# A smaller DMA scratch and a filler tile: the same instructions on SBUF tiles at other addresses

## The chip, the cores and the metric

One Trainium2 chip, one of its cores. The metric is device microseconds of one execution of the kernel; a profile of one execution stands beside the times.

## The reference, cut to what matters

```python
def reference(**kwargs):
    attn_out = _attn_ref(q, k, v, centroids)        # 2 x 8 heads, 768 x 64; a query sees the keys of its own cluster
    x = attn_out.transpose(0, 2, 1, 3).reshape(1536, 512)
    h = x @ w_in;  x = np.maximum(0.01 * h, h) @ w_out          # first MLP, 512 -> 2048 -> 512
    h = x @ w_in2; r = np.maximum(h, 0.0); return (r * r) @ w_out2   # second MLP
```

All in fp32; the weights come in as 64-bit floats.

## The kernel before, in words

**Two stages.** The first 240 us are the attention, unit by unit (`PLAN`, an order written out by hand for every engine). The rest is the two MLPs, `m = 0` and `m = 1`, and fills TensorE alone. The change issues nothing and moves nothing in the order, so what matters is which SBUF tiles the instructions of each stage read.

**The MLP stage.** The hidden width of 2048 is cut into 16 chunks `f` of 128. Each chunk has 1024 weights per partition: 512 of `w_in` and 512 of `w_out`. `decode_pieces(ci)` (`ci = 16 m + f`) loads a chunk into `wraw` (L124), turns it into fp32 on ScalarE and VectorE (`wt`, L131 to L148) and splits it into a high part `wh` (ScalarE, L159) and a low part `wl` (GpSimd, L160), each 128 x 1024 fp32r, 4096 bytes per partition. Three products (high x high, high x low, low x high) make up an fp32 product, so:

- `g1` (L728): for one chunk and one block of 512 tokens, 12 matmuls `h`, with a 128 x 128 slice of `wh` or `wl` as the stationary operand and 512 columns of `xh` or `xl` as the moving one.
- `act`: makes `gh` and `gl` from `h` on ScalarE and VectorE.
- `g2` (L770): 12 matmuls `o`. For `m = 0` a slice of `wh` or `wl` is stationary and `gh` or `gl` moves; for `m = 1` a slice of `gh` or `gl` is stationary and the 512 columns of `wh` or `wl` move.

Chunks go in groups (2, 2, 4, 4, 4 for `m = 0`, four times 4 for `m = 1`); each group runs over three token blocks. `g2` runs two units (`LAG = 2`) behind `g1`, so at a change of groups the two mix: 24 matmuls of the old group and 24 of the new one, by twelves.

**Where the weights lie.** `weights[m, f]` lie in a ring of eight places (`RING = 8`). Chunks with `ci % 8 < 4` go to the pool `wpx`, opened on the right side of SBUF while the attention still runs; the others go to `wpb`, on the left side. So **groups alternate**: four chunks in the upper buffers (`wpx`), four in the lower ones (`wpb`). 8 chunks of 16 in each MLP use the upper ones, which makes 8 x 3 x 24 = 576 matmuls per MLP, 1152 of the 2304 in all.

A pool on the right side grows down from the end of the memory, one on the left up from the DMA scratch and the constants. These are the addresses that the built program has for the tiles that TensorE reads and for a few others (bytes within a partition; "place" is the address modulo 4096):

| tile | side | address before | place |
|---|---|---|---|
| DMA scratch | left | 0 to 16384 | |
| `ident` | left | 16512 | 128 |
| `xh`, `xl` | left | 21600, 46176 | 1120 |
| `hb` (three) | left | 70752 to 107616 | 1120 |
| `gh`, `gl` (three each) | left | 78944 to 91232 | 1120, 3168 |
| lower `wh`, `wl` (four each, 4096 bytes apart) | left | 99424 to 132192 | 1120 |
| `vv` (two) | left | 107616, 113760 | 1120, 3168 |
| `e` (eight) | left | 119904 to 144480 | 1120, 96, 3168, 2144 |
| `eh`, `el` (two each) | left | 144480 to 169056 | 1120, 3168 |
| upper `wh`, `wl` (four each, 4096 bytes apart) | right | 184288 to 217056 | 4064 |
| `ds` | right | 184800 | 480 |
| `spl` (two) | right | 189408, 201696 | 992 |
| `rqk` (two) | right | 213984, 220128 | 992, 3040 |
| `rv` | right | 226272 | 992 |

(The right-side tiles of the attention and the upper weight buffers share their space one after the other, as do the left-side ones.)

All loads and stores are issued by SyncE (`nc.sync.dma_start`); no other engine issues a DMA.

Of the kernel before, what the change touches and what calls it, by code (L numbers as in the profile page):

```python
# [8 lines left out]
F32 = mybir.dt.float32  # L9
# [43 lines left out]
def attention_moe_moe_kernel(  # L53
# [9 lines left out]
    nc = tc.nc  # L63
# [18 lines left out]

    const = ctx.enter_context(tc.tile_pool(name="const", bufs=1))
    xp = ctx.enter_context(tc.tile_pool(name="xp", bufs=1))

    xh = xp.tile([128, HP, NT], F32R, name="xh")
    xl = xp.tile([128, HP, NT], F32R, name="xl")
# [590 lines left out]
    for u in range(-1, NU + 5):  # L678
# [8 lines left out]
        for op in PLAN[FIRST[u] if p == 0 else u % UPP].split():  # L687
            if ":" in op:
                name, lag = op.split(":")
# [5 lines left out]
            else:  # L695
                name, ahead = op.split("@")
# [184 lines left out]
```

## Time and profile before

| | us |
|---|---|
| median of 3 runs | 786.04 |
| lowest, highest | 784.79, 786.47 |
| span of the profiled execution | 782.9 |
| TensorE busy in it | 770.1 (98%) |
| VectorE, ScalarE, GpSimd busy | 532.2, 410.8, 293.4 |

The span runs from the first to the last instruction of the program on the core. Of the profiled execution only the span is recorded, no time as for the runs; the median of the runs is 3.1 us over it, the lowest run 1.9 and the highest 3.6. A busy TensorE is not TensorE at its peak: matmuls overlap, and a matmul's duration in a row (some 390 ns) is longer than the step from its start to the next one's start.

### The profile page before, as it was taken

The numbers are of one execution on the slowest core, as the hardware profiler recorded it, in microseconds if no ns is written. First come the engines' busy times: TensorE is split into PE (matmuls) and PEld (weight loads), VectorE is DVE, ScalarE is ACT, GpSimd is POOL, SyncE is SP. The second block draws the span as 40 slices with busy tenths as digits, with TensorE's granted clock in tenths as the row PEclk, the third lists the DMA queues.
The fourth block names the chain that finished last, engine by engine and source line by source line (L and its number), as shares of the span: only waits on it lengthen the run. The fifth ranks groups of instructions, "written<-read, shape, count | busy, mean of one in ns | idle before, by whom it ended". The sixth has DMA issues, their size and how long they took to land.

```text
span 782.9 us, 11015 instructions
## 1 busy us (share of the span) xinstructions
PE 770.1 (98%) x4147; PEld 665.3 (85%) x4147; DVE 532.2 (68%) x772; ACT 410.8 (52%) x759; POOL 293.4 (37%) x258
## 2 busy tenths in 40 slices
PE   8999999999999999999999999999999999999998
PEld 8899999999988888888888888888888888888886
DVE  5899999999998568775664577487257557533333
ACT  6988988988997563443442343445344234212121
POOL 2989889889765412221220214442022012100000
PEclk9999999999999999999999999999999999999999
DMA  7594574573502223233121113013113103000102
GB/s 224 121 205 110 105 180 108 113 164 78 139 1 93 96 85 108 105 107 108 55 107 54 33 75 108 1 54 108 55 54 108 54 0 108 1 0 1 52 17 95
DMA packets 16005, 66.35 MB, mean 85 GB/s; under 512 B 2704, under 2 KB 2704, under 8 KB 10960
## 3 DMA queue, kind: packets, MB, share of 16 engines
q1 hardware_dynamic: 15952, 65.64, 29.2%
q8 instruction: 33, 0.54, 0.3%
q14 instruction: 20, 0.16, 0.1%
HBM read 44.60 MB, written 3.15 MB: 61 GB/s over the span
## 4 chain that ended last, share of the span: by engine, by line
PE 82%; DVE 12%; ACT 4%; issue 1%; POOL 0%; DVEq 0%; ACTq 0%; POOLq 0%
PE o L770 34%; PE h L728 33%; PE A L451 5%; PE S L353 4%; DVE el L433 4%; PE T L416 4%; DVE nm L376 4%; ACT e L386 2%; DVE xt L473 1%; ACT eh L427 1%; DVE ds L279 1%; PE warm L202 1%; PE ohT L308 1%; DVE m L278 1%; PE S L257 1%
## 5 line engine op out<-in xcount | busy, mean ns | idle before, releaser
L160 POOL TENSOR_TENSOR wl<-wt,wh 128x1024 fp32r<-128x1024 f32 x32 | 77.5, 2423 | 297.1 <-ACT wh L159 246.6
L728 PE MATMUL h<-xl,wh 128*128 128x512 f32 x384 | 150.6, 392 | 0.0
L728 PE MATMUL h<-xh,wl 128*128 128x512 f32 x384 | 150.5, 392 | 0.0
L728 PE MATMUL h<-xh,wh 128*128 128x512 f32 x384 | 150.4, 393 | 0.0
L749 DVE TENSOR_TENSOR gl<-g,gh 128x512 fp32r<-128x512 f32 x96 | 91.6, 954 | 44.1 <-ACT gh L748 44.0
L748 ACT CAST gh<-g 128x512 fp32r<-128x512 f32 x96 | 59.6, 621 | 80.5 <-DVE g L745 42.2
L433 DVE TENSOR_TENSOR el<-T,eh 128x512 fp32r<-128x512 f32 x144 | 94.4, 683 | 5.6 <-ACT eh L427 3.7
L403 POOL TENSOR_SCALAR e<-e,r 128x768 f32<-128x768 f32 x96 | 88.5, 933 | 20.7 <-DVE r L400 13.4
L376 DVE TENSOR_REDUCE nm<-S 128x1 f32<-128x768 f32 x96 | 90.8, 947 | 4.6 <-PE S L257 2.3
L386 ACT ACTIVATE e<-S,nm 128x768 f32<-128x768 f32 x96 | 87.0, 906 | 11.1 <-DVE nm L376 6.8
L353 PE MATMUL S<-hb 128*128 128x384 f32 (+1 forms) x384 | 90.5, 350 | 1.6 <-ACT e L386 1.2
L745 DVE TENSOR_TENSOR g<-t 128x512 f32<-128x512 f32 x48 | 39.5, 822 | 73.3 <-ACT t L744 73.2
L744 ACT ACTIVATE t<-h 128x512 f32<-128x512 f32 x48 | 28.7, 598 | 113.3 <-PE h L728 113.2
L728 PEld LDWEIGHTS h<-xh,wl 128*128 128x128 f32 x384 | 72.3, 188 | 16.1
L728 PEld LDWEIGHTS h<-xl,wh 128*128 128x128 f32 x384 | 72.2, 188 | 16.0
L728 PEld LDWEIGHTS h<-xh,wh 128*128 128x128 f32 x384 | 72.2, 188 | 15.9
L427 ACT CAST eh<-T 128x512 fp32r<-128x512 f32 x144 | 79.4, 586 | 10.6 <-PE T L416 10.2
L451 PE MATMUL A<-eh,vv 128*128 128x256 f32 x288 | 79.5, 307 | 3.0 <-DVE xt L473 3.0
L416 PE MATMUL T<-ident,e 128*128 128x128 f32 x576 | 80.0, 274 | 1.1 <-DVE el L433 1.0
L770 PE MATMUL o<-gh,wl 128*128 128x512 f32 x192 | 75.4, 393 | 0.0
L770 PE MATMUL o<-gl,wh 128*128 128x512 f32 x192 | 75.3, 392 | 0.0
L770 PE MATMUL o<-wh,gl 128*128 128x512 f32 x192 | 75.3, 392 | 0.0
(106 smaller groups left out, 1407.0 us busy)
## 6 DMA issues: line engine op xcount, KB each, us to landing
wraw<-w SPq DMA_DIRECT2D x32, 1024.0 KB, 4.7
hb<-spl SPq DMA_DIRECT2D x14, 576.0 KB, 4.8
hb<-spl SPq DMA_DIRECT2D x42, 192.0 KB, 5.1
rqk<-qk SPq DMA_DIRECT2D x16, 384.0 KB, 4.5
rv<-v SPq DMA_DIRECT2D x8, 384.0 KB, 4.1
out<-ob SPq DMA_DIRECT2D x12, 256.0 KB, 2.1
twice<-qk SPq DMA_DIRECT2D x8, 192.0 KB, 6.0
hb<-st SPq DMA_DIRECT2D x28, 48.0 KB, 2.7
```

Source lines behind the costliest of these rows:

```text
L160: nc.gpsimd.tensor_tensor(out=wl, in0=t, in1=wh.bitcast(F32), op=ALU.subtract)
L353: nc.tensor.matmul(out=s[:, c, 0:HALF], lhsT=hb[0:k, a, i * 128 : (i + 1) * 128], rhs=hb[0:k, b, c * HALF : (c + 1) * HALF], start=(a == 0 ...
L376: nc.vector.tensor_reduce(out=n, in_=s_t[t][:, :, 0:HALF], axis=AX.XY, op=ALU.max, negate=True)
L386: nc.scalar.activation(out=e.rearrange("p (a b) -> p a b", a=2), in_=s_t.pop(t)[:, :, 0:HALF], func=AF.Exp, bias=n_t.pop(t), scale=1.0, ac ...
L403: nc.gpsimd.tensor_scalar(out=e_t[t], in0=e_t[t], scalar1=r_t[t // 2][:, t % 2 : t % 2 + 1], scalar2=1.0, op0=ALU.mult, op1=ALU.mult,)
L416: nc.tensor.transpose(T[:, o : o + 128], e_t[2 * u + b][:, kc * 128 : (kc + 1) * 128], ident)
L427: nc.scalar.copy(out=eh[:, 2 * g : 2 * g + 2, :].rearrange("p a b -> p (a b)"), in_=T_t[u, g])
L433: nc.vector.tensor_tensor(out=el[:, 2 * g : 2 * g + 2, :].rearrange("p a b -> p (a b)"), in0=T_t.pop((u, g)), in1=eh[:, 2 * g : 2 * g + 2, ...
L451: nc.tensor.matmul(out=A, lhsT=w, rhs=m[:, kc, :], start=(kc == 0 and i == 0), stop=(kc == KC - 1 and i == 1),)
L728: nc.tensor.matmul(out=h, lhsT=w[:, ws], rhs=x[:, kk, c], start=(kk == 0 and i == 0), stop=(kk == HP - 1 and i == 2),)
L749: nc.vector.tensor_tensor(out=gl, in0=g, in1=gh.bitcast(F32), op=ALU.subtract)
L770: nc.tensor.matmul(out=outs[o], lhsT=l, rhs=r, start=(first and i == 0), stop=(last and i == 2),)
```

## The change

Two edits. The DMA scratch at address 0 shrinks from 16384 to 4096 bytes per partition, so that every left-side tile lies 12288 bytes (three times 4096) lower. A tile of 736 fp32, 2944 bytes, that nothing writes or reads is allocated first on the right side, so that every right-side tile lies 2944 bytes lower.

```diff
     xp = ctx.enter_context(tc.tile_pool(name="xp", bufs=1))
+    rpad = ctx.enter_context(tc.tile_pool(name="rpad", bufs=1, side="right"))
+    rpad.tile([128, 736], F32, name="rp")
...
-    nc = bacc.Bacc("TRN2", target_bir_lowering=False, num_devices=1)
+    nc = bacc.Bacc("TRN2", target_bir_lowering=False, num_devices=1, dynamic_dma_scratch_size=4096)
```

On each of the five engines the same instructions stand in the same order with the same waits; only addresses differ. In the built program after the change:

| tile | address before, place | address after, place |
|---|---|---|
| every left-side tile | | 12288 lower, same place |
| upper `wh`, `wl` | 184288 to 217056, 4064 | 181344 to 214112, **1120** |
| lower `wh`, `wl` | 99424 to 132192, 1120 | 87136 to 119904, 1120 |
| `ds` | 184800, 480 | 181856, 1632 |
| `spl` | 189408 and 201696, 992 | 186464 and 198752, 2144 |
| `rqk` | 213984 and 220128, 992 and 3040 | 211040 and 217184, 2144 and 96 |
| `rv` | 226272, 992 | 223328, 2144 |

## Rows read from the trace of the kernel before

**Rows 1.** The page: busy time of each engine, granted clock by slice.
```profile
PE 770.1 (98%) x4147; PEld 665.3 (85%) x4147; DVE 532.2 (68%) x772; ACT 410.8 (52%) x759; POOL 293.4 (37%) x258
...
PEclk9999999999999999999999999999999999999999
```
**Rows 2.** Busy time by stretch, first row attention, then groups; us, busy (instructions), clock, DMA.
```profile
20.00:240.00 220.00, 214.68 (x1652) 207.53 (x1651) 205.44 (x368) 194.00 (x432) 185.48 (x177) 1.00 0.53 121
...
322.10:376.20 54.10, 54.10 (x240) 44.80 (x239) 34.03 (x46) 21.52 (x31) 12.02 (x5) 1.00 0.28 98
387.70:443.00 55.30, 55.30 (x240) 44.88 (x239) 30.05 (x40) 17.50 (x26) 7.21 (x3) 1.00 0.16 57
...
719.20:778.50 59.30, 59.30 (x263) 49.12 (x262) 21.53 (x33) 12.18 (x21) 0.00 (x0) 1.00 0.10 36
```
**Rows 3.** Timeline of TensorE, single matmuls: start us, duration us; first of each stretch.
```profile
241.42 0.47 PE L728 MATMUL h<-xh,wh 128*128 128x512 f32 x1
...
268.22 0.40 PE L770 MATMUL o<-gh,wh 128*128 128x512 f32 x1
...
310.98 0.39 PE L728 MATMUL h<-xh,wh 128*128 128x512 f32 x1
...
322.04 0.40 PE L728 MATMUL h<-xh,wh 128*128 128x512 f32 x1
...
376.47 0.40 PE L728 MATMUL h<-xh,wh 128*128 128x512 f32 x1
...
387.58 0.40 PE L728 MATMUL h<-xh,wh 128*128 128x512 f32 x1
...
443.37 0.40 PE L728 MATMUL h<-xh,wh 128*128 128x512 f32 x1
...
778.78 0.39 PE L770 MATMUL o<-wh,gl 128*128 128x512 f32 x1
```
**Rows 4.** Groups by line, 454.6 to 508.6 us (lower): count, busy us, mean ns, idle.
```profile
L728 PE MATMUL h<-xh,wl 128*128 128x512 f32 x40 | 15.6, 390 | 0.0
```
**Rows 5.** Groups by line, 387.7 to 443.0 us (upper, `m = 0`).
```profile
L728 PE MATMUL h<-xh,wl 128*128 128x512 f32 x40 | 15.8, 395 | 0.0
L770 PE MATMUL o<-gl,wh 128*128 128x512 f32 x40 | 15.8, 395 | 0.0
```
**Rows 6.** Groups by line, 652.4 to 707.7 us (upper, `m = 1`).
```profile
L770 PE MATMUL o<-wh,gl 128*128 128x512 f32 x40 | 15.8, 395 | 0.0
```
**Rows 7.** Timeline of TensorE, the attention's last `A` matmuls, 256 columns each.
```profile
256.12 0.28 PE L451 MATMUL A<-eh,vv 128*128 128x256 f32 x1
256.24 0.28 PE L451 MATMUL A<-el,vv 128*128 128x256 f32 x1
...
257.42 0.28 PE L451 MATMUL A<-el,vv 128*128 128x256 f32 x1
```
**Rows 8.** Groups by line, whole span: attention's TensorE work on right-side tiles, and `T`.
```profile
L416 PE MATMUL T<-ident,e 128*128 128x128 f32 x576 | 80.0, 274 | 1.1 <-DVE el L433 1.0
...
L257 PE MATMUL S<-cbd,rqk 128*128 128x32 f32 x144 | 19.0, 255 | 0.0
...
L308 PE MATMUL ohT<-ident,ds 128*64 128x128 f32 x42 | 6.9, 273 | 0.7 <-DVE r L400 0.4 <-ACT st L318 0.3
```
**Rows 9.** The page: DMA queues, and the weight loads with KB each and us to landing.
```profile
q1 hardware_dynamic: 15952, 65.64, 29.2%
...
wraw<-w SPq DMA_DIRECT2D x32, 1024.0 KB, 4.7
```
**Rows 10.** Timeline of GpSimd: the splits of `ci = 3` (first) and `ci = 7` (second).
```profile
272.69 2.41 POOL L160 TENSOR_TENSOR wl<-wt,wh 128x1024 fp32r<-128x1024 f32 x1 [6.40 <-ACT wh L159]
...
313.17 2.41 POOL L160 TENSOR_TENSOR wl<-wt,wh 128x1024 fp32r<-128x1024 f32 x1 [7.27 <-ACT wh L159]
```
**Rows 11.** Timeline of TensorE: first matmuls of chunks `ci = 3` and `ci = 7`.
```profile
280.31 0.39 PE L728 MATMUL h<-xh,wh 128*128 128x512 f32 x1
...
324.79 0.39 PE L728 MATMUL h<-xh,wh 128*128 128x512 f32 x1
```

## The prediction
> **What bounds the kernel now.** I read the busy times first: TensorE is busy for 770.1 of the 782.9 us span, at the full clock (2.4 GHz, a granted 1.0) in every slice [rows 1]. The busy times by stretch come next. In the attention, VectorE is nearly as busy as TensorE (205.4 and 214.7 of 220 us), so there a faster TensorE need not help. In the MLP stage TensorE is busy without a break and VectorE for 33 of 54 us at most [rows 2], so there the time is the number of matmuls times the step from one matmul's start to the next one's.
>
> That step is not the same everywhere. A group of four chunks has 4 x 3 x 24 = 288 matmuls; 24 at either end mix with a neighbouring group, and 240 stand alone. The timeline gives their time. The 240 that read the lower buffers run from 322.04 to 376.47: 54.43 us, **226.8 ns** a step. The 240 that read the upper ones run from 387.58 to 443.37: 55.79 us, **232.5 ns** [rows 3]. TensorE is idle in neither, and the clock is 1.00 in both [rows 2]. So an upper matmul costs 5.67 ns more, and 1152 of the 2304 are upper.
>
> I looked for another cause. Decoding is none: the last lower group has no decoding beside it (GpSimd at 0.00) and keeps up 263 matmuls in 59.3 us, the lower rate, while the lower stretch from 322.1 has GpSimd busy for 12 us [rows 2]. The role is none either: with the weights stationary the mean duration is 390 ns in a lower group and 395 in an upper one, for `h` and for `o` [rows 4, 5], and with the weights moving in the second MLP the upper group has 395 too [rows 6]. What is left is the buffers' address.
>
> **Which part of the address.** The change equalizes one thing: the place within 4096, 4064 for the upper buffers and 1120 for the lower ones. It leaves another: the upper ones stay some 90 KB further up. The eight lower buffers (`wh` and `wl`) lie 4096 apart and cover 32 KB without a hole, as the upper ones do, so no property that repeats every 8, 16 or 32 KB separates the two sets except the place within 4096. Against a plain boundary in the memory speaks `el` of the last attention unit, which lies at 162912 to 169056, above all lower weights and with a lower buffer's place. Eleven `A` steps of 256 columns take 257.42 - 256.12 = 1.30 us, 118 ns each [rows 7]. At 2.4 GHz 256 columns are 106.7 ns, so 11.5 ns are added; 512 columns are 213.3, to which a lower matmul adds 13.5 and an upper one 19.2. So `el` behaves as the lower buffers do. A boundary would have to lie in the 15 KB between 169056 and 184288.
>
> **The change, part by part.** Nothing is added, removed or moved in any engine's order or queue, SyncE's and GpSimd's included.
>
> *Upper weights at the lower ones' place.* I take the lower buffers' 226.8 ns for all upper matmuls.
> - From 310.98 on, 2304 - 264 = 2040 matmuls (the first two groups have 288, of which 24 come later) take 2039 steps up to the last start at 778.78: 467.80 us [rows 3]. At 226.8 ns they take 462.4. **Gain 5.4 us**: 888 upper matmuls by 5.67 ns are 5.0, and the rest are lower ones mixed with them.
> - Of the first 264, 80 lie ahead of 268.22, between the last attention units, and 184 behind it, where TensorE never waits [rows 3]. These give 184 x 5.67 = **1.0 us**. The 80 are worth 0.45, of which none or all may come through, since the attention's waits may absorb it; TensorE owns most of that stretch, so I take **0.45**.
>
> Sum: 5.4 + 1.0 + 0.45 = **6.9 us**. What could be late next? Not the engines that make `gh` and `gl`: they already keep up at 226.8 ns [rows 2]. The weights of `ci = 3` are ready at 275.10 and first used at 280.31 [rows 10, 11], and TensorE arrives there less than 1 us earlier; for `ci = 7` 9.2 us are left.
>
> *Attention tiles on the right.* `rqk` and `ds` change place too; TensorE reads them in 144 dot matmuls and 42 transposes of the units [rows 8]. At best each saves the upper surcharge: 186 x 5.67 = 1.1 us. At worst their new places cost that much. I take 0: the transposes of `ds` last 273 ns, those of `e`, which lies on the left, 274 [rows 8], so no surcharge shows, and VectorE nearly fills that stage.
>
> *The scratch.* All traffic of the program is on SyncE's queue, listed as hardware_dynamic; beside it stand only instruction loads [rows 9]. Nothing on GpSimd issues a DMA. I take 0, between nothing and the price of the slower rival.
>
> So the span becomes 782.9 - 6.9 = 776.0. That execution's span is 3.1 us under the median of the runs; I keep that and predict 786.04 - 6.86 = **779.2 us**.
>
> **A rule against it.** The upper matmuls with weights as the stationary operand (864 of the 1152) are as slow as those with weights moving (288) [rows 5, 6]. The Trainium skill, on the page "TensorE: Matmul & The Clock Gate", section "Step-by-step: what each phase is for", says that TensorE has two independent read ports, and that loading weights takes no read bandwidth from the running matmul. By that rule a stationary operand's address could not slow matmuls that hide the load, and only the 288 could gain; the trace disagrees, with 395 ns in either role.
>
> **The rivals.**
> - *Nothing happens: the cost belongs to the upper region, or to a distance between operands, not to the place.* For it: upper and lower have always differed in both. Against it: `el` above [rows 7]. The price is all of the gain: 786.0. The Trainium skill, "SBUF — State Buffer", section "Specifications (TRN2)", gives cachelines of 16 bytes and a penalty only for crossing to a new line. By it the places 4064 and 1120, both multiples of 16, are alike, and 786.0 would stay; the two rates in the trace show that some property of the address counts, not which. Chance 0.11.
> - *Only moving reads are cured*, and the stationary ones owe their surcharge to something else: 288 x 5.67 = 1.6, so 784.4. Against it: equal durations in both roles. Chance 0.02.
> - *Slower: the smaller scratch slows SyncE's transfers.* If their descriptors went through it, a 1 MB weight load, 4.7 us to landing now [rows 9], could take longer. One staging buffer makes the early chunks serial, so x us more per load have added up to 7x at `ci = 7`, where the split ends at 315.58 and the first use is at 324.79 [rows 10, 11]: 9.2 us of slack. The wait is 7x - 9.2 and eats the gain of 6.9 from x = 2.3. With landings doubled (x = 4.7) it is 23.7, and the time 786.0 - 6.9 + 23.7 = 802.8. Against it: the queue's kind. Chance 0.04.
>
> **How the numbers follow.** The forecast has the remaining 0.83. About 0.2% (1.6 us) can be told from no change here; the three runs span 1.7. The range goes down to 779.2 - 1.1 (attention) - 0.7 (a little under half of the runs' spread) = 777.4. Up, if only the stationary matmuls were cured, 864 x 5.67 = 4.9 gives 781.1, and with 0.7 it is 781.8; that covers the 0.45 that may be absorbed. Left out are the rivals with 0.17. Faster by over 0.2% (under 784.5): the forecast and half of the second rival, 0.84; the same: the first and the other half, 0.12; slower 0.04.
>
> **What would show it.** Right: 240 upper matmuls in 54.4 us instead of 55.8 at the same stretch of the program, 390 ns instead of 395 in their rows, lower groups as before, weight loads still 4.7 us to landing, and a last stretch that starts some 6.9 us earlier. Wrong: the upper groups still at 232 ns, or lower groups that have slowed, or a TensorE that now waits between 241 and 330 us.

## The result and the profile after

| | before | after |
|---|---|---|
| median, us | 785.79 (784.79 to 786.47, 4 runs) | 778.33 (777.83 to 779.4, 4 runs) |
| ratio, 95% interval | | 0.9912 [0.9898, 0.9926] |
| span of the profiled execution | 782.9 | 777.6 |

The kernel became 0.9% faster: 7.46 us between the medians, where 6.86 was forecast, and 778.33 us where 779.2 was. First the busy times by stretch of the changed kernel (us, then PE, PEld, DVE, ACT, POOL busy with their instructions, granted clock, DMA share, GB/s), for the stretches that answer to [rows 2] and two upper groups: the attention, a lower group, an upper one of the first MLP, an upper one of the second, the last lower one.

```profile
20.00:240.00 220.00, 214.61 (x1651) 207.83 (x1650) 205.69 (x366) 193.73 (x431) 185.13 (x175) 1.00 0.51 118
322.30:376.40 54.10, 54.10 (x241) 44.83 (x240) 35.55 (x47) 21.91 (x31) 12.03 (x5) 1.00 0.27 98
387.60:441.80 54.20, 54.20 (x241) 44.93 (x240) 30.23 (x40) 17.73 (x26) 7.18 (x3) 1.00 0.17 58
648.70:702.90 54.20, 54.20 (x241) 44.93 (x240) 27.50 (x37) 15.51 (x24) 4.79 (x2) 1.00 0.06 20
713.90:773.20 59.30, 59.30 (x263) 49.17 (x262) 21.60 (x34) 12.25 (x21) 0.00 (x0) 1.00 0.10 36
```

An upper group now has its 240 matmuls in the time of a lower one. The clock was 1.00 before and is 1.00 now, and the attention has not moved. The timeline of TensorE gives the steps to the hundredth (start us, duration us; the same matmuls of the program as in [rows 3]):

```profile
243.14 0.47 PE L730 MATMUL h<-xh,wh 128*128 128x512 f32 x1
...
269.59 0.39 PE L772 MATMUL o<-gh,wh 128*128 128x512 f32 x1
...
311.30 0.39 PE L730 MATMUL h<-xh,wh 128*128 128x512 f32 x1
...
322.18 0.39 PE L730 MATMUL h<-xh,wh 128*128 128x512 f32 x1
...
376.58 0.39 PE L730 MATMUL h<-xh,wh 128*128 128x512 f32 x1
...
387.46 0.39 PE L730 MATMUL h<-xh,wh 128*128 128x512 f32 x1
...
441.86 0.39 PE L730 MATMUL h<-xh,wh 128*128 128x512 f32 x1
...
773.47 0.39 PE L772 MATMUL o<-wh,gl 128*128 128x512 f32 x1
```

240 lower matmuls: 376.58 - 322.18 = 54.40 us; 240 upper ones: 441.86 - 387.46 = 54.40 us. Both are 226.7 ns a step, where the upper ones took 55.79 before [rows 3]. From the MLP stage's first matmul to its last it is 530.33 us, and it was 537.36: **7.03 us less**, in three parts:

| part | before | after | gain | forecast |
|---|---|---|---|---|
| first 80 matmuls, between attention units | 26.80 | 26.45 | 0.35 | 0.45 |
| next 184 | 42.76 | 41.71 | 1.05 | 1.04 |
| remaining 2039 steps | 467.80 | 462.17 | 5.63 | 5.4 |

The spans differ by 5.3 us only, because this execution's MLP stage began at 243.14 and that of before at 241.42. That start does not follow the change: in the twelve experiments below it lies between 241.10 and 243.16, in no order of the address (241.18 with the filler of the change alone). The profiled execution took 779.4 us as a whole, 1.8 over its span; by the same 1.8 the one of before took 784.7, about as long as its shortest run. The groups by line (count, busy us, mean ns, idle), first for the upper group of the first MLP, then for that of the second, answer to [rows 5, 6]:

```profile
L772 PE MATMUL o<-gl,wh 128*128 128x512 f32 x40 | 15.6, 390 | 0.0
L730 PE MATMUL h<-xh,wl 128*128 128x512 f32 x40 | 15.6, 389 | 0.0
```
```profile
L772 PE MATMUL o<-wh,gl 128*128 128x512 f32 x41 | 16.0, 390 | 0.0
```

395 has become 390 with the weights stationary and with the weights moving. The waits of TensorE from 243.2 to 770 us (who waited for whom: us in total, times, longest), and the weight loads:

```profile
PE A L453 <- DVE xt L475: 0.9, 1, 0.9
PE T L418 <- POOL e L405: 0.2, 1, 0.2
```
```profile
wraw<-w SPq DMA_DIRECT2D x32, 1024.0 KB, 4.7
```

Both waits belong to the attention's last units, which run between the first 80 matmuls; the 0.9 us was there before the change too. Behind them TensorE waits for nothing, and a load lands after 4.7 us as in [rows 9].

### The profile page after: what moved, and what is told of

Its sections match the earlier page's. It is cut to its first block, busy times and chain, and to the rows that moved or that the text cites. A ratio compares the mean times of both kernels' runs of the same rounds, so it can differ in the third digit from the quotient of the medians.

```text
span 777.6 us, 11015 instructions
## 1 busy us (share of the span) xinstructions
PE 763.9 (98%) x4147; PEld 665.9 (86%) x4147; DVE 533.2 (69%) x772; ACT 409.8 (53%) x759; POOL 293.4 (38%) x258
## 4 chain that ended last, share of the span: by engine, by line
PE 82%; DVE 11%; ACT 5%; issue 1%; POOL 0%; DVEq 0%; ACTq 0%; POOLq 0%
PE o L772 34%; PE h L730 33%; PE A L453 5%; PE S L355 4%; PE T L418 4%; DVE el L435 3%; DVE nm L378 3%; ACT e L388 3%; ACT eh L429 1%; DVE xt L475 1%; PE warm L204 1%; DVE ds L281 1%; PE ohT L310 1%; DVE m L280 1%; PE S L259 1%
## 5 line engine op out<-in xcount | busy, mean ns | idle before, releaser
L772 PE MATMUL o<-wl,gh 128*128 128x512 f32 x192 | 74.8, 390 | 0.0
```

The costliest lines, as they stand in the source:

```text
L772: nc.tensor.matmul(out=outs[o], lhsT=l, rhs=r, start=(first and i == 0), stop=(last and i == 2),)
```

## The experiments

Times are medians beside those of the kernel before on the same chip; a ratio has its 95% interval. The step is that of the 240 unmixed matmuls of an upper and a lower group of the first MLP (TensorE runs the same matmuls in all of these kernels, and in all but `e10_pattern_gl` in the same order; that trace also holds 11016 instructions in all, where the others hold 11015). Addresses are given modulo 256, which the runs turned out to call for: before, `xh`, `xl`, `gh`, `gl` and the lower weights lie at 96, the upper weights at 224.

| run | upper weights, mod 256 | others | upper step, ns | lower step, ns | us (before) | ratio |
|---|---|---|---|---|---|---|
| `e1_filler_only` | 96 | 96 | 226.7 | 226.7 | 777.83 (785.2) | 0.9906 [0.9886, 0.9925] |
| `e2_scratch_only` | 224 | 96 | 232.5 | 226.8 | 785.24 (785.2) | 1.0004 [0.9993, 1.0015] |
| `e3_left_384` | 224 | 224 | 226.7 | 226.7 | 777.94 (785.2) | 0.9903 [0.9884, 0.9923] |
| `e4_mid_384` | 96 | `xh`, `xl` 96; `gh`, `gl`, lower weights 224 | 230.3 | 230.4 | 787.08 (785.2) | 1.0021 [1.0012, 1.0031] |
| `e5_off_32` | 128 | 96 | 233.3 | 226.7 | 785.1 (785.17) | one run |
| `e11_off_64` | 160 | 96 | 233.3 | 226.8 | 786.13 (785.13) | one run |
| `e6_off_128` | 224 | 96 | 232.5 | 226.8 | 785.07 (785.17) | one run |
| `e7_off_256` | 96 | 96 | 226.7 | 226.7 | 778.08 (785.17) | one run |
| `e9_aligned_256` | 0 | 0 | 226.7 | 226.7 | 778.14 (785.13) | 0.9911 [0.9895, 0.9928] |
| `e8_pattern` | mixed | mixed | 231.1 | 227.8 | 786.67 (785.17) | one run |
| `e10_pattern_gl` | mixed | mixed | 231.3 | 232.0 | 788.4 (785.13) | one run |
| `e12_filler_128` | 96 | 96 | 226.7 | 226.7 | 777.74 (785.13) | 0.9911 [0.9894, 0.9927] |

### One half of the change at a time

`e1_filler_only` is the first hunk of the change without the second, `e2_scratch_only` the second without the first.

> The filler tile alone, with the DMA scratch left at 16384 bytes: the upper weight buffers lie at place 1120 modulo 4096, the left side stays where it was. My theory (the upper buffers' place is the whole cause): every matmul step of the MLP stage 226.7 ns, 240 matmuls of an upper group in 54.4 us instead of 55.8, time as with the full change, 778.3 us (777.5 to 779.5). Rival (the smaller scratch has a part in it): upper groups partly faster or the time over 780.

> The DMA scratch at 4096 bytes alone, no filler tile: the left side lies 12288 bytes lower at the same places, the upper weight buffers stay at place 4064. My theory: nothing changes, upper groups at 232.4 ns a step, lower ones at 226.7, 785.8 us, weight loads 4.7 us to landing. Rival (the scratch or the left side's absolute position counts): a time under 784.2 or over 787.4, or landing times that differ.

The filler has all of it: 0.9906, against 0.9912 for the whole change. The smaller scratch has nothing: 1.0004. The timeline of `e2_scratch_only`, first and last step of an upper group, still shows 444.25 - 388.46 = 55.79 us:

```profile
388.46 0.40 PE L728 MATMUL h<-xh,wh 128*128 128x512 f32 x1
...
444.25 0.40 PE L728 MATMUL h<-xh,wh 128*128 128x512 f32 x1
```

and its weight loads land after the same time:

```profile
wraw<-w SPq DMA_DIRECT2D x32, 1024.0 KB, 4.7
```

The scratch, and with it the position of all left-side tiles 12288 bytes up or down, is out as a cause.

### A place, or an agreement of two places?

The prediction spoke of the upper buffers' own place. Two buffers can also disagree. Here the upper ones stay where they were, and everything on the left moves by 384 bytes to meet them.

```diff
     const = ctx.enter_context(tc.tile_pool(name="const", bufs=1))
+    const.tile([128, 96], F32, name="lp")
```

> No filler, scratch as before; a pad of 384 bytes ahead of all left-side tiles puts xh, xl, gh, gl and the lower weights at place 1504 (480 modulo 512), where the upper weights (4064, also 480 modulo 512) already are modulo 512. Two theories: (relation) a matmul is slow where its two operands lie at different places modulo 512, so now every step is 226.7 ns and the time about 778.3 us. (own place) a tile at 480 modulo 512 is slow by itself, so now all 2304 matmuls take 232.4 ns, 13 us over the changed kernel, about 791.5 us, and lower groups are as slow as upper ones. If only lengths of 4096 count (1504 against 4064), upper stays at 232.4 and lower at 226.7, 785.8 us.

Agreement it is. The timeline of `e3_left_384`, start of a lower group, start of the mixed part behind it, and the same of an upper group:

```profile
321.32 0.39 PE L729 MATMUL h<-xh,wh 128*128 128x512 f32 x1
...
375.72 0.39 PE L729 MATMUL h<-xh,wh 128*128 128x512 f32 x1
...
386.60 0.39 PE L729 MATMUL h<-xh,wh 128*128 128x512 f32 x1
...
441.00 0.39 PE L729 MATMUL h<-xh,wh 128*128 128x512 f32 x1
```

54.40 us for either, with the upper buffers at their old, slow place. So neither that place nor the upper region is slow by itself.

`e4_mid_384` makes all four cases at once: the filler of the change, and 384 bytes between `xl` and what follows on the left.

```diff
     xl = xp.tile([128, HP, NT], F32R, name="xl")
+    xp.tile([128, 96], F32, name="mp")
```

> Filler tile (upper weights at place 1120, 96 modulo 512) and a pad of 384 bytes behind xh and xl, which moves gh, gl and the lower weights to 480 modulo 512 while xh and xl stay at 96. Four cases in one run. Relation theory: h in upper groups fast (226.7), h in lower groups slow (232.4), o in upper groups slow, o in lower groups fast; 1152 slow ones, about 785 us. Own-place theory: only h in upper groups is fast, 1728 slow ones, about 788 us. Region theory (upper always slow, lower always fast) is out if upper h runs at 226.7.

The groups by line of its upper group, 388.4 to 443.4 us:

```profile
L773 PE MATMUL o<-gh,wh 128*128 128x512 f32 x40 | 15.8, 394 | 0.0
...
L731 PE MATMUL h<-xl,wh 128*128 128x512 f32 x40 | 15.6, 391 | 0.0
```

and of its lower group, 322.2 to 377.2 us:

```profile
L731 PE MATMUL h<-xh,wl 128*128 128x512 f32 x40 | 15.8, 394 | 0.0
...
L773 PE MATMUL o<-gh,wh 128*128 128x512 f32 x40 | 15.6, 390 | 0.0
```

The slow one is `o` in the upper group (`gh` at 224, weights at 96) and `h` in the lower one (`xh` at 96, weights at 224); where both are at 96 or both at 224, the duration is 390 or 391. The own-place theory wanted `o` in the lower group slow. The time, 787.08 us, is 2 us more than the relation theory's 785 and lies nearer to the own-place theory's 788; it is the durations by kind that decide between them. Inside a group the trace has `h` and `o` in turn, mostly twelve at a time, some in runs of 2 to 14. By its start times, which are finer than the rows, the first three fast steps behind a slow run still take 231 to 233 ns, and only then 226 or 227. So the unmixed steps are 230.3 and 230.4, where half of 226.7 and half of 232.5 would be 229.6; over 2304 matmuls the difference is those 2 us.

### How far off, and what repeats

Three fillers that put the upper weights 32, 64 and 128 bytes off, and one that puts them 256 off; the diff of `e7_off_256`, the others differ in the number (728, 720, 704):

```diff
+    rpad = ctx.enter_context(tc.tile_pool(name="rpad", bufs=1, side="right"))
+    rpad.tile([128, 672], F32, name="rp")
```

> Filler of 2912 bytes: the upper weights lie 32 bytes off the places (modulo 512) of xh, xl, gh and gl, at 128 against 96. If any offset modulo 512 counts alike, upper steps are 232.4 ns and the time about 785; if only some distance or a coarser line counts, they are at 226.7 and the time about 778; an offset that parts the reads better than none could also be faster than 226.7. Lower groups 226.7.

> Filler of 2880 bytes: the upper weights lie 64 bytes off modulo 256. 32 off gave 233.4 ns, 128 off 232.4. If any disagreement counts alike, 232 to 234 ns, about 785 us; lower groups 226.7.

> Filler of 2816 bytes: the upper weights lie 128 bytes off modulo 512. The kernel before is 384 off, which is 128 modulo 256. If the pattern repeats every 256 bytes, upper steps are 232.4 ns here and the time about 785, as before; if it repeats every 512 and depends on the distance, another value.

> Filler of 2688 bytes: the upper weights lie 256 bytes off modulo 512, and not at all modulo 256. If the pattern repeats every 256 bytes, or every 128 (which the 384 of before excludes), upper steps are 226.7 ns and the time about 778; if it repeats every 512, they are slow, 232 ns or so, and the time about 785.

The upper group of `e6_off_128` (443.70 - 387.91 = 55.79 us) and of `e7_off_256` (440.54 - 386.14 = 54.40 us):

```profile
387.91 0.40 PE L730 MATMUL h<-xh,wh 128*128 128x512 f32 x1
...
443.70 0.40 PE L730 MATMUL h<-xh,wh 128*128 128x512 f32 x1
```
```profile
386.14 0.39 PE L730 MATMUL h<-xh,wh 128*128 128x512 f32 x1
...
440.54 0.39 PE L730 MATMUL h<-xh,wh 128*128 128x512 f32 x1
```

So the pattern repeats every 256 bytes: 256 off is no offset at all, 128 off costs what the 384 of before did, and 32 and 64 off cost a little more (233.3 ns). None of the offsets tried is better than none; under 32 bytes none was tried.

`e9_aligned_256` (`const.tile([128, 40], F32, name="lp")` on the left, a filler of 56 fp32 on the right) asks whether a start on a multiple of 256 is worth something by itself.

> A pad of 160 bytes ahead of the left side and a filler of 224 bytes on the right: all operands of the MLP matmuls start at multiples of 256. If only the agreement of the two operands modulo 256 counts, every step is 226.7 ns as in the changed kernel, about 778 us. If a start on a 256-byte line is worth something by itself, steps fall under 226.7 (512 columns at 2.4 GHz are 213.3) and the time under 776.

It is not: 226.7 ns at 0, as at 96 and at 224. `e12_filler_128` is a much smaller change that should do: `rpad.tile([128, 32], F32, name="rp")` and nothing else.

> The smallest form that the runs so far suggest: a filler tile of 128 bytes and nothing else. The upper weights lie at place 3936 modulo 4096, far from the lower ones' 1120, but at 96 modulo 256 as these do. If agreement modulo 256 is all that counts, every step of the MLP stage is 226.7 ns and the time that of the full change, about 778 us. If the place within 4096 counts beyond that, upper steps are over 227 ns and the time over 779.5.

```profile
385.65 0.39 PE L730 MATMUL h<-xh,wh 128*128 128x512 f32 x1
...
440.05 0.39 PE L730 MATMUL h<-xh,wh 128*128 128x512 f32 x1
```

440.05 - 385.65 = 54.40 us again, and 0.9911 [0.9894, 0.9927]: 128 bytes of filler give what the change gives with 2944 of filler and 12288 of scratch. No version was faster than that.

### Which two operands: open

While a matmul runs, the weights of the next one are loaded. In the changed kernel the load (PEld, 0.19 us) of the weights for `xh`, `wl` starts with the matmul ahead of it (start us, duration us):

```profile
399.93 0.39 PE L730 MATMUL h<-xl,wh 128*128 128x512 f32 x1
399.93 0.19 PEld L730 LDWEIGHTS h<-xh,wl 128*128 128x128 f32 x1
```

So a moving operand can disagree with the weights of its own matmul, or with those loaded beside it (in the expectations: the same-matmul theory and the overlap theory). `e8_pattern` puts `xl` and the upper `wl` at 224 and leaves the rest at 96, so that in `h` of an upper group every moving operand agrees with the weights loaded beside it, but two of three disagree with their own.

```diff
+    xp.tile([128, 96], F32, name="mp")
     xl = xp.tile([128, HP, NT], F32R, name="xl")
+    xp.tile([128, 32], F32, name="mq")
...
+            if ci == 0:
+                pool.tile([128, 96], F32, tag="wp", name="wp", bufs=1)
             wl = pool.tile([128, 2 * DM], F32R, tag="wl", name="wl")
```

> Which two operands must agree: those of one matmul, or the moving one of a matmul and the weights loaded during it for the next. Modulo 512, xh lies at 96 and xl at 480, upper wh at 96 and upper wl at 480, everything else at 96. The order in h is wh with xh, wh with xl, wl with xh. Overlap theory: in h of upper groups each moving operand is beside a load of the same place (xh with wh, xl with wl, xh with wh), so h in upper groups is fast, 226.7 ns, up to 228.5 by what the o blocks between leave behind. Same-matmul theory: two of three pairs differ, so h in upper groups takes 230.5 ns. In lower groups one pair of three differs by either theory, h about 228.6 ns; o in upper groups of the first MLP likewise.

`e10_pattern_gl` adds `gl` at 224 by the same two pads around it in `gp`, so that `o` follows the pattern too. TensorE's matmuls stand in another order in places there.

> The pattern again, now without slow blocks between in the upper groups: modulo 256 xl, gl and upper wl lie at 224, all other operands of the MLP matmuls at 96. Overlap theory (the moving operand of a matmul must agree with the weights loaded for the next): in upper groups all reads agree, h and o at 226.7 ns; in lower groups one of three differs, 228.6 to 232. Same-matmul theory: in upper groups two of three pairs differ, 230.5 to 232.5 ns, and lower groups, with one of three, are the faster ones.

Neither theory fits both runs. In `e8_pattern` the step behind an `h` of an upper group is 230.0 ns on average, by the trace's start times: near the 230.5 of the same-matmul theory, and over the 228.5 that the overlap theory allowed. But the step behind an `o` is 232.2 there, where both theories have one disagreement in three and expected some 228.6. By kind, in the rows of 389.3 to 444.6 us, `xl` with `wh` lasts 395 ns although it agrees with the `wl` loaded beside it, and `xh` with `wl` only 390 although it disagrees. In `e10_pattern_gl` the upper groups are slow (231.3), against the overlap theory. The same-matmul theory wanted the lower groups faster: in the first MLP they are not (232.0), in the second they are by a little (230.3, and 231.2 for the upper ones).

The lower groups say more. In that of `e8_pattern` (first MLP, 323.6 to 378.1 us) all weights lie at 96, so `xl` with `wh` is the one pair of three in `h` that disagrees. It alone is slow:

```profile
L732 PE MATMUL h<-xl,wh 128*128 128x512 f32 x40 | 15.8, 395 | 0.0
L732 PE MATMUL h<-xh,wh 128*128 128x512 f32 x40 | 15.6, 389 | 0.0
```

In `e10_pattern_gl` the `h` of the lower groups has the same places modulo 256. In the first MLP (322.2 to 377.7 us) `xh` with `wh` is slow there too, in the second (589.0 to 644.2 us) it is not:

```profile
L732 PE MATMUL h<-xh,wh 128*128 128x512 f32 x40 | 15.8, 395 | 0.0
```
```profile
L781 PE MATMUL o<-wh,gl 128*128 128x512 f32 x41 | 16.3, 397 | 0.0
L732 PE MATMUL h<-xh,wh 128*128 128x512 f32 x41 | 16.0, 390 | 0.0
L781 PE MATMUL o<-wl,gh 128*128 128x512 f32 x40 | 15.8, 396 | 0.0
```

In that second group `o` of `wh` and `gl` disagrees in itself, and `o` of `wl` and `gh` only with the `gl` that is loaded beside it; both are slow. So neither pair alone explains all rows, and the same kind of matmul at the same places modulo 256 lasts 389 or 395 ns from one group to another; what ran ahead of it seems to count too, which no run tests by itself. A mix is slow, from 227.8 ns up to nearly the full surcharge, although part of the pairs agree. Between which two reads the disagreement counts stays open.

## Why the prediction was right, and where its words were not

- **The bound and the sum.** VectorE's most in an MLP stretch of [rows 2] is 34.0 of 54.1 us, where the prediction reads 33; that changes nothing, as TensorE has no break beside it. TensorE's step times the number of matmuls set the time, and all of the gain is in the step: 7.03 us in the MLP stage against 6.86. The small excess is in the last part, 5.63 for 5.4: a lower step is 226.7 now, where the stretch taken as the rate [rows 3], 226.8, still had a few disturbed ones from the mixed part ahead of it. The other 0.4 of the 7.46 lies within the interval (5.8 to 8.0 us).
- **The 80 matmuls between attention units** gave 0.35 of 0.45; what took the rest is not shown.
- **The attention tiles and the scratch**, both costed at nothing: `e2_scratch_only` shows it for the scratch. For the attention, the matmuls on `rqk` and `ds` last as long as in [rows 8] (255 and 273 ns), and in the six kernels with all steps at 226.7 the MLP stage is 7.0 to 7.1 us shorter and the median 7.0 to 7.5, which leaves the attention some tenths at most. The start of the MLP stage wanders by 2 us between executions, so one trace could not show them.
- **The median.** 3.1 us were taken as what lies around a span; the runs show 1.8. The execution of before that was profiled was simply short. The error did no harm, since it is the gain that was taken from the median of before. That median fell from 786.04 to 785.79 with a fourth run, which is 0.25 of the 0.87 us by which the forecast was high.
- **The argument on the address** led to the right number by words that were too narrow. "The place within 4096" was one of several descriptions that the trace could not part, because the change makes the upper buffers equal to the lower ones in all of them. The runs part them: it is no place, but an agreement of the two operands of the matmul stream modulo 256 (`e3_left_384`, `e7_off_256`, `e12_filler_128`). The prediction had set "a distance between operands" against the place, and counted it among the reasons for which nothing would happen; it is a distance that counts, modulo 256. That the number came right all the same was luck in this step: on both sides of the change `xh`, `gh` and the lower weights share one place modulo 256, and putting the upper weights at the lower ones' place within 4096 makes them agree with all of these. The evidence of `el` [rows 7] fits this too: `el` and `vv` both lie at 96 modulo 256.
- **The rivals.** Nothing-happens, by a region or a line of 16 bytes, is out: in `e3_left_384` the old addresses of the upper buffers are fast. Offsets of 32, 64 and 128 bytes, all multiples of 16, are slow (232.5 to 233.3 ns). The line of 16 bytes in the Trainium skill ("SBUF — State Buffer", section "Specifications (TRN2)") does not tell these from 0. Only-moving-reads is out, since every kind of upper matmul now takes 389 or 390. The Trainium skill ("TensorE: Matmul & The Clock Gate", section "Step-by-step: what each phase is for") states two independent read ports, so that a weight load takes no read bandwidth from the running matmul. In the traces the step depends on both operands' addresses, 232.5 ns for 226.7 when they disagree modulo 256; which read waits is not shown, so whether the ports are at fault stays open. The slower rival needed longer transfers, and they stayed at 4.7 us.

## What to carry to other kernels

Where TensorE is busy without a break, look at the step from start to start, group by group: two groups of the same shape with different steps point to their tiles. If the only difference is which tiles they read, compare the addresses of the stationary and the moving operand modulo 256, and make them agree with a pad of less than 256 bytes per pool; here 128 bytes were worth 0.9%. All of this was measured with fp32r matmuls of 512 columns and a weight load for each; other types and sizes were not tried. Before a change is explained by the property it was made for, move the other side to meet it: one pad on the left told agreement from place.

## What the runs showed of the hardware that was not expected

- Matmuls of 512 fp32r columns step at 226.67 ns (2039 steps in 462.17 us) when both operands agree modulo 256, whatever the common place (0, 96, 224), and at 232.0 to 233.3 ns when all disagree (232.0 and 232.2 in the second MLP of the kernel before). At 2.4 GHz 226.67 ns are 544 clock cycles, 32 more than there are columns.
- The surcharge is no fixed amount per matmul. By the start times, the steps of an upper group of the first MLP before run from 227 to 242 ns in a series that repeats every seven matmuls; with 32 bytes off (`e5_off_32`), 235 takes turns with 231 or 232.
- The disagreement can last beyond its matmuls: mixed streams keep most of the surcharge in `e10_pattern_gl` (231.3 and 232.0 ns), and behind twelve disagreeing matmuls the first three agreeing ones are still slow (`e4_mid_384`). It need not: in the lower groups of `e8_pattern` the surcharge stays with the one kind that disagrees, at 227.8 ns a step in all.
